# Four alternating transformer layers: logits moved from TensorE to VectorE, and the blocks ordered as a wavefront

## The chip, the cores and the metric

The kernel runs on one core of one Trainium2 chip. The metric is the device time in microseconds of one execution; the time before is the median of three runs. The profile shows one execution, whose span runs from its first to its last instruction.

## The reference

The input x has 2048 tokens of 1024 features (bf16). Four layers follow each other, A, B, A, B, with the same weights in both A and in both B layers; each adds its result to x. The core of the two:

```python
def _A_ref(x, wqkv, wo):              # x is layer-normed
    H = 32; Dh = D // H               # 32 heads of 32
    W, dil = 8, 2
    q, k, v = ...  (x @ wqkv), split by head
    idx = pos[:, None] - (arange(W) * dil)[None, :]
    ...
    logits = einsum("bhsd,bhswd->bhsw", q, kg) * Dh ** -0.5
    logits = where(idx >= 0, logits, -1e9)
    o = einsum("bhsw,bhswd->bhsd", softmax(logits), vg)
    return o @ wo

def _B_ref(x, W_gate, W_up, W_down):  # F = 3584
    return (relu(x @ W_gate) * (x @ W_up)) @ W_down
```

Each token looks at itself and at seven earlier ones, two tokens apart, in each of 32 heads.

## The kernel before

x stays in SBUF as 16 tiles of 128 tokens. The work is cut into 4 blocks of 512 tokens (BLK), four tiles each, and goes layer by layer, block by block within a layer: 16 items (L, b). `merge` interleaves the steps of an item with those deferred from earlier items by fractions of the item (SCHED 3), and the framework turns the result into one instruction stream per engine, each of which runs in order. All loads of weights, transposes and round trips are issued on SyncE (SP), whose queue waits in order too.

An A item has 24 projections `proj(c, q|k|v)`, each 8 matmuls of 128x128 by 128x512 into one PSUM bank (L316), copied to SBUF by ScalarE (ACT). q and k stay on chip with features on the partitions. For each chunk c of 128 features VectorE (DVE) multiplies q by k at the eight shifts in one instruction of 4096 elements (L345), and `red(c)` sums over the features of each head on TensorE (PE): eight matmuls with a stationary matrix `wide` of ones (L358), into a two-bank PSUM tile. The softmax is on DVE and ACT (L373 to L382). Only v goes out to DRAM (`v_d`) and comes back head-major (`vhm`, L428): 32 heads by four groups of 128 tokens on the partitions, 32 features and 142 tokens along the row. `pv(g)` (L440 to L443) forms the weighted sum of v on DVE for four features at a time. Its result goes out to `o_d` and comes back as `oT`, for wo (L471), whose result DVE adds to x (L478). wqkv is loaded once per block, in rows of 512 B (L302).

A B item has 28 steps `gu(j)`: eight matmuls for the gate, relu by ACT into one of three buffers r (L518), eight matmuls for up (L513), and on DVE the product of the two, hT (L519). Then come 224 down matmuls (L543), and DVE adds their sums to x. Weights pass through a ring of five slabs of 1 MB.

Layer-norm: ACT forms the sums and the normalised rows (L186, L187, L210), DVE and GpSimd (POOL) the small steps, and one transposing DMA on SP makes xnT (L214). PSUM has six banks for matmul results and two for the logits. The numbers in names follow layer and block: hT_3_5098 is of the fourth block, block 3.

Of the kernel before, what the change touches and what calls it, by code (L numbers as in the profile page):

```python
# [11 lines left out]
AX = mybir.AxisListType  # L12
# [13 lines left out]
SLAB = 512  # L26

# [5 lines left out]
def _interleave(a, b):  # L33
    out = []
    na, nb = len(a), len(b)
    if na == 0:
        return list(b)
    if nb == 0:
        return list(a)
    ia = ib = 0  # L40
    while ia < na or ib < nb:
        if ib >= nb or (ia < na and ia * nb <= ib * na):
            out.append(a[ia]); ia += 1
        else:
            out.append(b[ib]); ib += 1
    return out
# [3 lines left out]
def kernel(  # L50
# [28 lines left out]
    import os as _os0  # L79
    _os_env = _os0.environ  # L80
# [3 lines left out]
    wring = ctx.enter_context(tc.tile_pool(name="wring", bufs=int(_os_env.get("KRING", "5"))))  # L84
    xnT_pool = ctx.enter_context(tc.tile_pool(name="xnT", bufs=2))
    ln_pool = ctx.enter_context(tc.tile_pool(name="ln", bufs=2))
    stat_pool = ctx.enter_context(tc.tile_pool(name="stat", bufs=2))
    tl_pool = ctx.enter_context(tc.tile_pool(name="tl", bufs=1))
    a_pool = ctx.enter_context(tc.tile_pool(name="attn", bufs=2))
    psum = ctx.enter_context(tc.tile_pool(name="psum", bufs=int(_os_env.get("KACC", "6")), space=bass.MemoryType.PSUM))  # L90
    psum_l = ctx.enter_context(tc.tile_pool(name="psum_l", bufs=int(_os_env.get("KLB", "1")), space=bass.MemoryType.PSUM))
# [5 lines left out]
    wide = const.tile([P, 60], BF16, name="wide")  # L97
    nc.gpsimd.memset(wide[:], 0.0)
    for hl in range(4):
        nc.gpsimd.memset(wide[32 * hl:32 * hl + 32, 28 + hl:29 + hl], 1.0)  # L100
# [4 lines left out]
    neg_half = const.tile([P, TPB], F32, name="neg_half")  # L105
    nc.gpsimd.memset(neg_half[:], -0.5)
    NTOK = HALO + S
    v_d = dram.tile([H * DH, NTOK], BF16, name="v_d")
    o_d = dram.tile([NT, H, DH, P], BF16, name="o_d")
    zpad = const.tile([P, KC, HALO], BF16, name="zpad")  # L110
    nc.gpsimd.memset(zpad[:], 0.0)
    nc.sync.dma_start(bass.AP(tensor=v_d.tensor, offset=v_d.offset, ap=[[NTOK, P], [P * NTOK, KC], [1, HALO]]), zpad[:])

    x_tiles = []
    for t in range(NT):
        xt = xpool.tile([P, D], BF16, name=f"x{t}")
        x_tiles.append(xt)
# [3 lines left out]
    def load_x_steps(b):  # L121
        def f(t):
            return lambda: nc.sync.dma_start(x_tiles[t][:], x_dram[t * P:(t + 1) * P, :])
        return [f(t) for t in range(b * TPB, (b + 1) * TPB)]

    import os as _os
    KNOB = {
        "red2": int(_os.environ.get("KRED2", "0")),
        "wo_lo": float(_os.environ.get("KWO_LO", "0.3")),
        "wo_hi": float(_os.environ.get("KWO_HI", "0.7")),  # L130
        "p2_lo": float(_os.environ.get("KP2_LO", "0.0")),
        "ln_lo": float(_os.environ.get("KLN_LO", "0.25")),
        "ln_hi": float(_os.environ.get("KLN_HI", "0.95")),
        "bq": _os.environ.get("KBQ", "sync"),
        "dt": int(_os.environ.get("KDT", "1")),
        "hp": int(_os.environ.get("KHP", "0")),
    }
    bq = {"sync": nc.sync, "act": nc.scalar, "pool": nc.gpsimd}[KNOB["bq"]]
    from contextlib import nullcontext as _nullctx

    def hp():
        return tc.high_priority() if KNOB["hp"] else _nullctx()
    _dbg_on = bool(_os.environ.get("KDEBUG"))

    def dbg(name, ap_):
        if not _dbg_on:
            return
        shp = list(ap_.shape)
        if name.startswith("ps_"):
            tmp = const.tile(shp, ap_.dtype, name=f"dbgtmp_{name}")  # L150
            nc.vector.tensor_copy(tmp[:], ap_)
            ap_ = tmp[:]
        h = nc.dram_tensor(f"dbg_{name}", shp, ap_.dtype, kind="ExternalOutput")
        nc.sync.dma_start(h.ap(), ap_)
# [8 lines left out]
    def lnt_steps(item):  # L163
        L, b = item
        holder = {}
        steps = []

        def alloc():
            holder["xnT"] = xnT_pool.tile([P, TPB, KC, P], BF16, tag="xnT", name=f"xnT_{L}_{b}")
            holder["st"] = stat_pool.tile([P, 2, TPB], F32, tag="st", name=f"st_{L}_{b}")  # L170

        def stats(t):
            def f():
                if t == 0:
                    alloc()
                    if KNOB["dt"]:
                        holder["xn_all"] = ln_pool.tile([P, TPB, D], BF16, tag="xn_all", name="xn_all", bufs=1)
                st = holder["st"]
                xt = x_tiles[b * TPB + t]
                if KNOB["dt"]:  # L180
                    junk = holder["xn_all"][:, t, :]
                    junk2 = junk
                else:
                    junk = ln_pool.tile([P, D], BF16, tag="junk", name="junk", bufs=1)[:]
                    junk2 = ln_pool.tile([P, D], BF16, tag="junk", name="junk2", bufs=1)[:]
                nc.scalar.activation(junk, xt[:], ACT.Identity, accum_out=st[:, 0, t:t + 1])  # L186
                nc.scalar.activation(junk2, xt[:], ACT.Square, accum_out=st[:, 1, t:t + 1])  # L187
            return f

        def small():  # L190
            st = holder["st"]
# [11 lines left out]
            holder["rstd"], holder["nb"] = rstd, nb  # L203

        def do_tr(t):
            def f():
                xt = x_tiles[b * TPB + t]
                if KNOB["dt"]:
                    xna = holder["xn_all"]
                    nc.scalar.activation(xna[:, t, :], xt[:], ACT.Identity, scale=holder["rstd"][:, t:t + 1],  # L210
                                         bias=holder["nb"][:, t:t + 1])
                    if t == TPB - 1:
                        xnT = holder["xnT"]
                        nc.sync.dma_start_transpose(xnT[:].rearrange("p t k n -> p (t k) n"),  # L214
                                                    xna[:].rearrange("p t d -> p (t d)"))
                    return
                xn = ln_pool.tile([P, D], BF16, tag="xn", name="xn")
                nc.scalar.activation(xn[:], xt[:], ACT.Identity, scale=holder["rstd"][:, t:t + 1],
                                     bias=holder["nb"][:, t:t + 1])
                tp = psum.tile([P, KC, P], BF16, tag="acc", name="tp")  # L220
                for c in range(KC):
                    nc.tensor.transpose(tp[:, c, :], xn[:, c * P:(c + 1) * P], ident[:])
                nc.scalar.copy(holder["xnT"][:, t, :, :], tp[:])
# [464 lines left out]
```

## Time and profile before

| | |
|---|---|
| time of three runs | 1686.22, 1688.92 and 1688.09 us, median 1688.09 |
| span of the profiled execution | 1682.7 us; its own time is not given apart from that, and the median of the runs is 5.4 us above it |
| granted clock of TensorE | 0.999 |
| busy: PE, DVE, ACT, POOL | 1648.5, 726.0, 452.9, 21.0 us |
| DMA engines busy, share | 64.3% of the span for the main queue |
| HBM read, written | 265.16 MB, 21.00 MB |

Read it from the engine that sets the end: busy shares say how full each engine is over the span, the strips of 40 slices say where, and the waits say who holds whom. Where an engine has much idle time in one layer and none in another, its share over the whole span tells little.

### The profile page before, as it was taken

How to read it: one execution, taken by the hardware profiler on the slowest of the kernel's cores; microseconds unless marked ns; L12 is line 12 of the kernel's file. 1: busy time of each engine (PE TensorE's matmuls, PEld its weight loads, DVE VectorE, ACT ScalarE, POOL GpSimd, SP SyncE). 2: the span in 40 equal slices, each digit the busy share in tenths (PEclk: the TensorE clock that was granted, in tenths of full speed). 3: DMA queues.
4: the chain of work that ended last, by engine and by line, in shares of the span. 5: the costliest groups of instructions: out<-in, count | busy, mean ns of one | idle time of the engine just before them, and what ended most of it. 6: DMA issues, size and time to landing. Idle time of an engine off the chain costs nothing.

```text
span 1682.7 us, 18808 instructions
## 1 busy us (share of the span) xinstructions
PE 1648.5 (98%) x7906; PEld 734.2 (44%) x7968; DVE 726.0 (43%) x873; ACT 452.9 (27%) x737; POOL 21.0 (1%) x40
## 2 busy tenths in 40 slices
PE   7999999999999999999999999999999999999998
PEld 3343434444444444444444334444444444444444
DVE  3589889562211221111135999796422112211111
ACT  6642433201410153211325335141014002300110
POOL 1000000000000000000000000000000000000000
PEclk9999999999999999999999999999999999999999
DMA  9987877854655366444759787968538455555442
GB/s 274 209 190 194 209 210 193 235 189 161 167 172 167 120 206 180 139 150 150 189 148 213 182 195 183 249 171 237 198 123 245 142 164 173 163 163 175 150 156 70
DMA packets 435013, 303.11 MB, mean 180 GB/s; under 512 B 134897, under 2 KB 429809, under 8 KB 433905
## 3 DMA queue, kind: packets, MB, share of 16 engines
q1 hardware_dynamic: 434640, 301.39, 64.3%
q8 instruction: 62, 1.02, 0.3%
q10 hardware_dynamic: 288, 0.52, 0.1%
q14 instruction: 23, 0.18, 0.0%
HBM read 265.16 MB, written 21.00 MB: 170 GB/s over the span
## 4 chain that ended last, share of the span: by engine, by line
PE 84%; DVE 7%; ACT 3%; DMA 3%; issue 2%; POOL 0%; SPq 0%; ACTq 0%; DVEq 0%; POOLq 0%
PE acc_g L513 23%; PE acc_u L513 22%; PE acc_wo L471 7%; PE acc_q L316 3%; PE acc_v L316 3%; PE acc_k L316 3%; ACT xn_all L210 1%; ACT xn_all L187 1%; ACT xn_all L186 1%; DMA xnT_2_6641<-xn_all 1%; DMA xnT_2_872<-xn_all 1%; DVE ssum L378 0%; DMA xnT_1_453<-xn_all 0%; DMA xnT_0_1818<-xn_all 0%; DMA xnT_0_7583<-xn_all 0%
## 5 line engine op out<-in xcount | busy, mean ns | idle before, releaser
L518 ACT ACTIVATE r<-acc_g 128x512 bf16<-128x512 f32 x224 | 132.7, 594 | 829.2 <-PE acc_g L513 797.8
L519 DVE TENSOR_TENSOR hT_3_10875<-acc_u,r 128x512 bf16<-128x512 f32 x28 | 19.4, 692 | 77.4 <-PE acc_u L513 77.4
L519 DVE TENSOR_TENSOR hT_3_5098<-acc_u,r 128x512 bf16<-128x512 f32 x28 | 19.4, 692 | 77.4 <-PE acc_u L513 77.4
L519 DVE TENSOR_TENSOR hT_1_8821<-acc_u,r 128x512 bf16<-128x512 f32 x28 | 19.4, 691 | 74.0 <-PE acc_u L513 69.1
L519 DVE TENSOR_TENSOR hT_2_9861<-acc_u,r 128x512 bf16<-128x512 f32 x28 | 19.4, 691 | 74.0 <-PE acc_u L513 69.1
L519 DVE TENSOR_TENSOR hT_1_3052<-acc_u,r 128x512 bf16<-128x512 f32 x28 | 19.4, 691 | 74.0 <-PE acc_u L513 69.1
L519 DVE TENSOR_TENSOR hT_2_4088<-acc_u,r 128x512 bf16<-128x512 f32 x28 | 19.4, 691 | 68.1 <-PE acc_u L513 56.4
L200 POOL TENSOR_TENSOR rstd<-vpe,neg_half 128x4 f32<-128x4 f32 x15 | 16.8, 1119 | 1413.7 <-DVE vpe L198 1279.7
L543 PEld LDWEIGHTS <-hT_3_10875 128*128 128x128 bf16 x224 | 21.9, 98 | 26.4
L543 PEld LDWEIGHTS <-hT_2_4088 128*128 128x128 bf16 x224 | 21.9, 98 | 26.4
L543 PEld LDWEIGHTS <-hT_0_7781 128*128 128x128 bf16 x224 | 21.9, 98 | 26.4
L543 PEld LDWEIGHTS <-hT_1_8821 128*128 128x128 bf16 x224 | 21.9, 98 | 26.4
L543 PEld LDWEIGHTS <-hT_2_9861 128*128 128x128 bf16 x224 | 21.9, 98 | 26.4
L543 PEld LDWEIGHTS <-hT_0_2016 128*128 128x128 bf16 x224 | 21.9, 98 | 26.4
L543 PEld LDWEIGHTS <-hT_1_3052 128*128 128x128 bf16 x224 | 21.9, 98 | 26.4
L543 PEld LDWEIGHTS <-hT_3_5098 128*128 128x128 bf16 x224 | 21.9, 98 | 26.4
L519 DVE TENSOR_TENSOR hT_0_2016<-acc_u,r 128x512 bf16<-128x512 f32 x28 | 19.0, 686 | 28.3 <-PE acc_u L513 25.9
L519 DVE TENSOR_TENSOR hT_0_7781<-acc_u,r 128x512 bf16<-128x512 f32 x28 | 19.0, 686 | 28.3 <-PE acc_u L513 25.9
L358 PEld LDWEIGHTS <-wide 128*32 128x32 bf16 x512 | 9.4, 94 | 35.1 <-issue 31.6
L378 DVE TENSOR_REDUCE ssum<-d 128x128 f32<-128x1024 f32 x8 | 15.3, 1908 | 1.9 <-ACT d L376 1.9
L277 PE MATMUL tp<-ident,xn_all 128*128 128x128 bf16 x32 | 4.0, 311 | 10.0 <-DVE xn_all L255 8.7
L376 ACT ACTIVATE d<-d 128x1024 f32<-128x1024 f32 x8 | 8.5, 1058 | 14.6 <-DVE d L375 14.6
(1513 smaller groups left out, 3291.3 us busy)
## 6 DMA issues: line engine op xcount, KB each, us to landing
vhm_0_734<-v_d SPq DMA_DIRECT2D x4, 284.0 KB, 7.1
vhm_1_1664<-v_d SPq DMA_DIRECT2D x4, 284.0 KB, 7.4
vhm_2_2287<-v_d SPq DMA_DIRECT2D x4, 284.0 KB, 8.9
vhm_3_3323<-v_d SPq DMA_DIRECT2D x4, 284.0 KB, 9.9
vhm_0_6503<-v_d SPq DMA_DIRECT2D x4, 284.0 KB, 6.7
vhm_1_7429<-v_d SPq DMA_DIRECT2D x4, 284.0 KB, 6.7
vhm_2_8052<-v_d SPq DMA_DIRECT2D x4, 284.0 KB, 8.3
vhm_3_9092<-v_d SPq DMA_DIRECT2D x4, 284.0 KB, 10.4
```

What stands on the lines that cost most here:

```text
L186: nc.scalar.activation(junk, xt[:], ACT.Identity, accum_out=st[:, 0, t:t + 1])
L187: nc.scalar.activation(junk2, xt[:], ACT.Square, accum_out=st[:, 1, t:t + 1])
L200: nc.gpsimd.tensor_tensor(rstd[:], vpe[:], neg_half[:], op=ALU.pow)
L210: nc.scalar.activation(xna[:, t, :], xt[:], ACT.Identity, scale=holder["rstd"][:, t:t + 1], bias=holder["nb"][:, t:t + 1])
L316: nc.tensor.matmul(acc[:], lhsT=wsl[:, kc, wcol:wcol + P], rhs=xnT[:, :, kc, :], start=(kc == 0), stop=(kc == KC - 1))
L358: nc.tensor.matmul(Lt[32 * tq:32 * tq + 32, 4 * wh:4 * wh + 4, :], lhsT=wide[:, 28 - 4 * c:60 - 4 * c], rhs=prod[:, 4 * wh:4 * wh + 4, tq ...
L378: nc.vector.tensor_reduce(ssum[:], d[:].rearrange("p w t -> p t w"), axis=AX.X, op=ALU.add)
L471: nc.tensor.matmul(acc[:], lhsT=oTa[:, c, t, :], rhs=wsl[:, c, :], start=(c == 0), stop=(c == KC - 1 and not res_pe))
L513: nc.tensor.matmul(acc[:], lhsT=slabs[nm][:, kc, jl * P:(jl + 1) * P], rhs=xnT[:, :, kc, :], start=(kc == 0), stop=(kc == KC - 1))
L518: nc.scalar.activation(r[:], acc[:], ACT.Relu)
L519: nc.vector.tensor_tensor(hT[:, j, :], accs["u"][:], r[:], op=ALU.mult)
L543: nc.tensor.matmul(ac[t], lhsT=hT[:, j, t * P:(t + 1) * P], rhs=wsl[:, jl, :], start=(j == 0), stop=(j == FC - 1))
```

## The change

The kernel is written anew around the same tiles. In the diff:

- q, k and v are all staged by ACT (`stage`, two buffers of two chunks), stored to DRAM per block (`q_d`, `k_d`, `v_d`; the last 14 tokens also into the next block's rows), and read back head-major (`load`, L292: four DMAs each).
- The logits are on DVE alone: for each shift w one multiply of 4096 elements (`mul`) and a tree of six adds with f32 results over the 32 features (`tree`). `wide`, `red` and their 512 matmuls go, and with them the two PSUM banks: eight banks are now for matmul results.
- The max and the sum of the softmax are trees of three instructions in place of one reduction each.
- `Plan` sorts all steps by planned times, kept by a clock for PE (`plan.pe`, 0.216 us a matmul) and one for DVE (`plan.dve`). The order on PE is a wavefront: the projections of layer 0, with wo(0,0) in the middle of the last; then for each b gate_up(1,b), wo(0,b+1) or wo(2,0), down(1,b) and, from b = 1, proj(2,b-1); then gate_up(3,0), proj(2,3), wo(2,1), down(3,0), gate_up(3,1), wo(2,2), down(3,1), gate_up(3,2), wo(2,3), down(3,2), gate_up(3,3), down(3,3).
- In layer 0 the six 1 MB slabs of wqkv are loaded once and stay in the ring (`w0`), which now has six buffers. In layer 2 they are loaded per block, in rows of 1 KB.
- xnT and oT share one pool `tpose` of three buffers.

The core of the diff (`+` is the changed kernel, `-` the one before):

```diff
-    wring = ctx.enter_context(tc.tile_pool(name="wring", bufs=int(_os_env.get("KRING", "5"))))
+    wring = ctx.enter_context(tc.tile_pool(name="wring", bufs=6))
+    tpose = ctx.enter_context(tc.tile_pool(name="tpose", bufs=3))
+    psum = ctx.enter_context(tc.tile_pool(name="psum", bufs=8, space=bass.MemoryType.PSUM))
...
-        def red(c):
-            def f():
-                prod = st.pop(("prod", c))
...
-                        nc.tensor.matmul(Lt[32 * tq:32 * tq + 32, 4 * wh:4 * wh + 4, :],
-                                         lhsT=wide[:, 28 - 4 * c:60 - 4 * c],
...
+    def plan_proj(plan, L, b, ready, between=None):
...
+                    if L == 0:
+                        if b == 0:
+                            w0[(nm, g)] = load_slab(wqkv_v[:, :, col0:col0 + SLAB], f"w{nm}_{L}_{g}")
+                        hold["w"] = w0[(nm, g)]
...
+                nc.scalar.copy(s[:, j % 2, :], acc[:])
+                if j % 2 == 1:
...
+                    if nm == "q":
+                        dst = _dram(q_d[b], f0 * BLK, [[BLK, P], [P * BLK, 2], [1, BLK]])
+                        nc.sync.dma_start(dst, s[:])
...
+    def plan_attn(plan, L, b, ends, pace):
+        def load(nm, src, row, n):
+            def f():
+                t = hm_pool.tile([P, DH, n], BF16, tag=nm, name=f"{nm}hm_{L}_{b}")
+                for tq in range(TPB):
+                    nc.sync.dma_start(t[32 * tq:32 * tq + 32, :, :],
+                                      _dram(src[b], tq * P, [[DH * row, H], [row, DH], [1, n]]))
...
+        def mul(w):
...
+                nc.vector.tensor_tensor(pr[:], st["q"][:], _ap(st["k"], HALO - DIL * w, [[HALO + P, DH], [1, P]]),
+                                        op=ALU.mult)
...
+        def tree(w):
+            def f():
+                pr = st.pop(("pr", w))
+                l1 = at_pool.tile([P, 8, P], F32, tag="l1", name="l1")
+                nc.vector.tensor_tensor(l1[:], pr[:, 0:8], pr[:, 8:16], op=ALU.add)
+                nc.vector.tensor_tensor(l1[:], l1[:], pr[:, 16:24], op=ALU.add)
+                nc.vector.tensor_tensor(l1[:], l1[:], pr[:, 24:32], op=ALU.add)
+                for n in (4, 2):
+                    nc.vector.tensor_tensor(l1[:, 0:n], l1[:, 0:n], l1[:, n:2 * n], op=ALU.add)
+                nc.vector.tensor_tensor(st["L"][:, w, :], l1[:, 0], l1[:, 1], op=ALU.add)
...
+        q0 = max(ends["k"] + 0.5, plan.dve - 45.0)
+        plan.at(q0, load("q", q_d, BLK, P))
+        plan.at(q0, load("k", k_d, ROW, HALO + P))
+        plan.at(max(ends["v"] + 0.5, plan.dve), load("v", v_d, ROW, HALO + P))
+        t = max(plan.dve, ends["k"] + T_BOUNCE)
+        for w in range(0, W, 2):
+            plan.at(t, mul(w))
+            plan.at(t + 2.2 * pace, mul(w + 1))
+            plan.at(t + 4.4 * pace, tree(w))
+            plan.at(t + 9.0 * pace, tree(w + 1))
+            t += 13.6 * pace
...
+    for b in range(NB):
+        if b + 1 < NB:
+            ln(0, b + 1, [plan.pe + 14.0 + 2.6 * t for t in range(TPB)])
+        proj(0, b, between=(lambda: wo(0, 0)) if b == NB - 1 else None)
+    for b in range(NB):
+        gate_up(1, b)
+        if b + 1 < NB:
+            wo(0, b + 1)
+        else:
+            wo(2, 0)
+        down(1, b)
+        if b >= 1:
+            proj(2, b - 1)
+    for b in range(NB):
+        gate_up(3, b)
+        if b == 0:
+            proj(2, NB - 1)
+        if b + 1 < NB:
+            wo(2, b + 1)
+        down(3, b)
+    plan.run()
```

`gu`, `down`, `wo`, `pv` and the layer-norm keep their instructions; the hT multiply is now L437, the adds to x L400 (wo) and L464 (down), r still has three buffers.

## The prediction

> **What bounds the kernel now.** I read the page's first, second and fourth parts, then windows by stage, then the waits, then the rows that price the new work.
>
> ```profile
> PE 1648.5 (98%) x7906; PEld 734.2 (44%) x7968; DVE 726.0 (43%) x873; ACT 452.9 (27%) x737; POOL 21.0 (1%) x40
> ...
> PE   7999999999999999999999999999999999999998
> ...
> DVE  3589889562211221111135999796422112211111
> ...
> DMA  9987877854655366444759787968538455555442
> ...
> PE 84%; DVE 7%; ACT 3%; DMA 3%; issue 2%; POOL 0%; SPq 0%; ACTq 0%; DVEq 0%; POOLq 0%
> ```
>
> TensorE sets the time: 98% busy and 84% of the chain. VectorE is full only in slices 2 to 8 and 20 to 27 of 40, the two attention layers, and idle in between. The windows answer says the same with numbers (columns: stretch, length, busy of PE, PEld, DVE, ACT, POOL, clock, DMA share, GB/s):
>
> ```profile
> 100.00:140.00 40.00, 37.81 (x201) 16.12 (x194) 40.00 (x34) 11.14 (x19) 0.00 (x0) 1.00 0.88 203
> ...
> 380.00:860.00 480.00, 478.84 (x2208) 217.35 (x2229) 96.78 (x158) 117.87 (x190) 5.04 (x5) 1.00 0.54 163
> ```
>
> In attention both engines are full; in the GLU layer PE misses 1.2 us of 480. The waits say why PE is not held there: VectorE waits for PE at all 28 hT multiplies, never PE for it.
>
> ```profile
> DVE hT_3_5098 L519 <- PE acc_u L513: 77.4, 28, 3.1
> ...
> PE acc_g L513 <- DMA xnT_0_1818<-xn_all: 2.2, 1, 2.2
> ```
>
> **TensorE's floor.** Eight matmuls of 512 columns take 1.73 us in the chain, 0.216 each. The 7424 that stay make 1604 us: a projection block 41.5, wo 13.8, gate_up 96.8 (28 steps j of 3.456), down 48.4. With the start (first matmul at 15.05, its first eight 3.56, so 16.9 in effect) and 4.1 after the last one: 1625. The span of before is 1682.7: some 35 more for the 64 logit reductions (PE's busy 1648.5 less 1604, less 4.0 of transposes and 5 of the slow start; 0.55 each) and 23 of waits. The change takes the 35 away; that is its sure gain, and the waits could go too. The medians of the shown runs lie 5.4 above this span; I add 5.4 to every span, supposing that what lies around it stays.
>
> **What VectorE gets.** Rows of before:
>
> ```profile
> L345 DVE TENSOR_TENSOR prod_251<-q_237,k_0_0_248 x1: 2293/2293/2293, 21.8 to 21.8; 128x4096 bf16<-128x4096 bf16 x1
> ...
> L375 DVE TENSOR_TENSOR d<-L_0_305,m x1: 1224/1224/1224, 68.2 to 68.2; 128x1024 f32<-128x1024 f32 x1
> ...
> L382 DVE TENSOR_TENSOR a_0_631<-d,rs x1: 1224/1224/1224, 75.3 to 75.3; 128x1024 bf16<-128x1024 f32 x1
> ...
> L441 DVE TENSOR_TENSOR t_800<-t_800 x1: 1217/1217/1217, 106.3 to 106.3; 128x2048 bf16<-128x2048 bf16 x1
> ...
> L519 DVE TENSOR_TENSOR hT_3_5098<-acc_u,r 128x512 bf16<-128x512 f32 x28 | 19.4, 692 | 77.4 <-PE acc_u L513 77.4
> ```
>
> One offset w costs a 4096 multiply as before (2.2 from start to start), and now a tree: three adds of 1024 with an f32 side, then f32 adds of 512, 256 and 128. 1024 and 512 have rows (1.22, 0.69); the line through them gives 0.43 and 0.29. With 0.03 for each start behind its own result the tree is 5.2 and the offset 7.45. The first add (bf16 in, f32 out) has no row: it lies between 0.68 (the 1024 bf16 add) and 1.22; I take 1.22 by L382, the nearest mixed form; the other end saves 8 x 0.54 = 4 us a block. The Trainium skill, "VectorE: DVE Perf Modes", "What auto-detection actually checks", speaks against the f32 tree: the double rate needs every tensor 16-bit. By it 1.22 holds and the sum stays; against it, 4 a block would go.
>
> Per block: 8 x 7.45 = 60, softmax 8 (3.7 of trees, subtract, reciprocal 0.95, multiply, the wait for exp), pv 8 x 4.27 = 34: 100 to 102, bounds 95 and 104. Before it was about 60. The total rises from 726 to about 1060 us, 63% of the span: enough room on average, so the question is where it lies.
>
> **Where it lies.** VectorE runs in order. In the built program each attention of blocks (0,1) to (2,2) stands inside one gate_up phase, between its hT multiplies; down and projection have 12.6 us of VectorE in 90. From the first hT multiply to the last, gate_up offers 27 x 3.456 = 93.3. VectorE's rows there sum to 98.7 in (1,0), 104.4 in (1,1), 120 in (1,2), (1,3) and (3,0), and 18.5 in (3,2) and (3,3), with 92 ahead of the first hT in (3,1). TensorE cannot run on: r has 3 buffers and PSUM 8 banks, so it leads by four j, 14 us, and then waits.
>
> For (1,2), (1,3), (3,0), T being the start of the projection before: its k load stands on SP behind the transpose of the next layer-norm, whose buffer (three shared by xnT and oT) comes free with the projection's last matmul, T + 41.5. The queue rows:
>
> ```profile
> 66.93 7.78 SPq L214 DMA_TRANSPOSE xnT_2_872<-xn_all  x1
> 74.80 5.08 SPq L428 DMA_DIRECT2D vhm_0_734<-v_d  x4
> ...
> vhm_0_734<-v_d SPq DMA_DIRECT2D x4, 284.0 KB, 7.1
> ```
>
> 7.8 for the transpose, 5.1 for four loads, 7 to land: k is there at T + 63. hT1 to hT4 are done by then; from there to hT24 the rows sum to 104 (between hT8 and hT9 alone 27.5), so T + 167; u28, which needs hT24's bank, ends at T + 168.5 instead of T + 138.3. With attention at 100 rather than 102, +29 each; if k is never late, VectorE starts after hT4 at T + 55: +20; with later loads +36.
>
> Layer 0 is alike. Before starts gate_up(1,0) at 224; the floor is 16.9 + 4 x 41.5 + 13.8 = 196.6. Attention (0,0) waits for k stored (chunks end 44.6, landing 8), 10 us of queue for q and k and 7 to land: 67, so it ends about 168, beside layer-norm steps. o out (4.0), oT back (6.6) and what SP has between (some 10) put wo(0,0) at 190, ending 204. (PE is free from about 179: the floor's 162 for three and a half projections, and 17 lost in block 1, where the layer-norm step of block 3 stands behind attention on VectorE, its transpose on SP, and the stores behind that.) Its residual adds stand behind seven offsets of attention (0,1), 168 + 52 = 220; the eight banks hold wo's sums, so the last half of proj(0,3) (20.7) waits for them: 241, then the layer-norm transpose: gate_up(1,0) at 250, bounds 235 and 260: +53 (+38 to +63).
>
> The rest: (1,0) starts 8 late on VectorE and has 5 too much: +8 (3 to 12). (1,1): 11 too much, hT1 up to 11 late, less a lead: +15 (8 to 20). (3,1): attention (2,3) starts 7.5 after wo(2,1); 92 us stand before hT1, 25 more to hT8, which frees the bank of j = 12: 121 to 125 against 90 at the floor: +30 (20 to 38).
>
> Weights: wqkv in layer 0 goes three times less over DMA (3 x 12288 packets of 512 B at 32 ns, over 16 engines: 74 us), 1-KB rows in layer 2 save 23; the q and k round trips add 21 a block (by the packet records: 4096 of 256 B at 22 ns and as many of 284 B at 34, 2048 of 1 KB at 52, over 16): 168. Net +71, to some 1150 busy of 1820: off the path on average. ACT's copies stay equal in number; each of 0.59 hides beside 1.73 of matmul; if not, 24 a block would come.
>
> **Sum.** 1625 + 53 + 8 + 15 + 3 x 29 + 30 = 1818 span, 1823 as a time. Low ends: 1625 + 38 + 3 + 8 + 60 + 20 + 5 = 1759; high ends: 1625 + 63 + 12 + 20 + 108 + 38 + 5 = 1871.
>
> **Rivals.**
> *VectorE keeps ahead* (faster). If hT multiplies are served in time, PE loses the reductions and most waits: 1625 + 15 to 25 in layer 0 + 5 = 1645 to 1655. For it: 63% of VectorE on average. Against: the order is fixed, and 120 does not fit into 93 plus a lead of 14. It decides if attention takes under about 80 a block. 0.12.
> *Only part of the lateness reaches PE.* Layer 0 as forecast at its low end, the three phases at 5 to 15, (3,1) absorbed: 1700 to 1759. For it: the lead may be longer, and k may land before hT4. 0.17.
> *The queue starves PE.* Stores that wait for ACT or VectorE block SP, and slabs come late in all of layers 1 to 3, as in the window of 88% DMA share: 2 us at each of the 35 slab pairs of the five gate_up phases that hold attention adds 70: 1893, spread 1871 to 1940. For it: all of it on SP, 256-B packets. Against: 54% share in GLU. The Trainium skill, "DMA: Bandwidth & Descriptors", "Specifications", says that packets under 512 B miss the line rate, the direction of these rows (22 ns for 256 B, 52 for 1 KB). Chance 0.10.
> *Gains and losses cancel*: 0.02. Forecast, 1759 to 1871: 0.59.
>
> A measurement of this kernel tells about 0.2% from no change. Range 1725 to 1895, which leaves out the fast case, the near end of the second and the far end of the third. Faster 0.12, same 0.02, slower 0.86.
>
> **What would show it.** Right: PE's strip dips in gate_up of (1,2), (1,3), (3,0); waits of acc_u or acc_g on the hT multiply or relu, near 30 us a phase; no idle VectorE from k's landing to hT28; gate_up(1,0) near 250; attention about 100 of VectorE a block. The layer-0 step is wrong if wo's adds are not late; the forecast is wrong if PE is over 95% busy, or if PE waits for slabs rather than for VectorE.

## The result, and the profile after

The changed kernel takes 1822.91 us (median of four runs, 1821.95 to 1825.6); the kernel before takes 1687.15 (median of four, 1685.18 to 1688.92). The ratio is 1.0808, with a 95% interval of 1.0793 to 1.0823: slower by 136 us. The forecast was 1823, range 1725 to 1895.

The profile page of the changed kernel, the parts that were shown of before (busy time, strips, chain):

```profile
PE 1640.1 (90%) x7407; PEld 734.8 (40%) x7456; DVE 1024.4 (56%) x1225; ACT 447.2 (25%) x737; POOL 20.8 (1%) x35
...
PE   7779689969899987999879998799679999999999
...
DVE  1599988989991049920599105991896211221111
...
DMA  9848688646857695476953969539837465456541
...
PE 61%; DVE 27%; DMA 4%; issue 3%; ACT 2%; SPq 2%; POOL 0%; DVEq 0%; POOLq 0%; ACTq 0%
```

TensorE falls from 98 to 90% of the span, and its share of the chain from 84 to 61%; VectorE's rises from 7 to 27%. VectorE's strip shows five separate hills (slices 2 to 12, 15 to 17, 20 to 22, 25 to 27 and 29 to 31), and TensorE's strip dips at each. After slice 32 VectorE is nearly idle and TensorE full: there is no attention left. VectorE is busy 56% on average, so its share of the span explains nothing.

The windows answer of the changed kernel, for gate_up(1,2) with its attention and for a stretch without attention (columns as before: stretch, length, busy of PE, PEld, DVE, ACT, POOL, clock, DMA share, GB/s):

```profile
645.00:766.00 121.00, 100.96 (x450) 44.43 (x449) 103.70 (x113) 19.10 (x32) 0.00 (x0) 0.93 0.71 169
...
1512.00:1768.00 256.00, 255.69 (x1182) 115.84 (x1187) 51.23 (x78) 46.71 (x76) 1.01 (x1) 1.00 0.52 161
```

The waits of TensorE in the changed kernel (engine, what waited, releaser: us in total, times, longest):

```profile
PE acc_u L432 <- DVE hT L437: 38.3, 8, 11.3
PE dacc L458 <- DMA wd<-in_B_W_down_dram: 32.6, 2, 17.5
PE acc_u L432 <- DMA wu<-in_B_W_up_dram: 19.8, 5, 7.7
PE acc_g L432 <- DVE x L464: 11.9, 1, 11.9
PE acc_k L253 <- ACT stage_k L255: 11.4, 1, 11.4
PE acc_k L253 <- DVE x L400: 9.4, 1, 9.4
...
PE acc_g L432 <- DMA xnT<-xn_all: 8.7, 1, 8.7
PE acc_g L432 <- DMA wg<-in_B_W_gate_dram: 7.3, 1, 7.3
```

Before, TensorE hardly waited for anyone in GLU; now it does, and for two parties of like weight. Over the whole kernel, what VectorE releases late (hT, x, and 6.9 put down to the tree at L311) is 66.5 us; weight slabs that land late (wd, wu, wg, and 6.1 for wo) are 65.8. The 6.9 is probably a slab too: it ends 8.5 us after the issue of wu, at the place in (1,3) where (1,2) and (3,0) end their waits for wu 8.9 and 8.6 us after its issue. Then it is 59.6 for VectorE and 72.7 for slabs. Staging by ACT adds 20.5, the transpose 8.7.

### The profile page after: what moved, and what is told of

The parts are those of the page before. It is cut to its first block, busy times and chain, and to the rows that moved or that the text cites. A ratio compares the mean times of both kernels' runs of the same rounds, so it can differ in the third digit from the quotient of the medians.

```text
span 1820.3 us, 18488 instructions
## 1 busy us (share of the span) xinstructions
PE 1640.1 (90%) x7407; PEld 734.8 (40%) x7456; DVE 1024.4 (56%) x1225; ACT 447.2 (25%) x737; POOL 20.8 (1%) x35
## 2 busy tenths in 40 slices
DMA packets 468277, 319.07 MB, mean 175 GB/s; under 512 B 216288, under 2 KB 460000, under 8 KB 468192
## 4 chain that ended last, share of the span: by engine, by line
PE 61%; DVE 27%; DMA 4%; issue 3%; ACT 2%; SPq 2%; POOL 0%; DVEq 0%; POOLq 0%; ACTq 0%
PE dacc L458 17%; PE acc_u L432 15%; PE acc_g L432 14%; DVE pr L302 5%; PE acc_wo L397 4%; PE acc_q L253 4%; PE acc_k L253 3%; DVE l L312 3%; DVE l L313 3%; DVE l L311 3%; PE acc_v L253 3%; DVE pvt L349 3%; DVE l L315 3%; DVE hT L437 2%; DMA khm<-k_d 1%
## 5 line engine op out<-in xcount | busy, mean ns | idle before, releaser
L432 PE MATMUL acc_u<-xnT,wu 128*128 128x512 bf16 x1792 | 435.8, 388 | 65.1 <-DVE hT L437 38.3
L432 PE MATMUL acc_g<-xnT,wg 128*128 128x512 bf16 x1792 | 429.9, 384 | 27.9 <-DVE x L464 11.9
L458 PE MATMUL dacc<-wd,hT 128*128 128x512 bf16 x1759 | 390.5, 382 | 34.5 <-DMA wd<-in_B_W_down_dram 32.6
L437 DVE TENSOR_TENSOR hT<-acc_u,r 128x512 bf16<-128x512 f32 x224 | 153.7, 687 | 348.6 <-PE acc_u L432 348.6
L432 PEld LDWEIGHTS <-wu 128*128 128x128 bf16 x1792 | 177.1, 99 | 289.0 <-issue 56.2
L458 PEld LDWEIGHTS <-hT 128*128 128x128 bf16 x1792 | 175.8, 98 | 247.8 <-issue 23.1
L432 PEld LDWEIGHTS <-wg 128*128 128x128 bf16 x1792 | 176.6, 99 | 245.6 <-issue 30.8
L464 DVE TENSOR_TENSOR x<-dacc,x 128x512 bf16<-128x512 f32 x64 | 43.4, 690 | 223.7 <-PE dacc L458 223.7
L302 DVE TENSOR_TENSOR pr<-qhm,khm 128x4096 bf16<-128x4096 bf16 x64 | 145.7, 2286 | 17.6 <-DMA v_d<-stage_v 10.4
L349 DVE TENSOR_TENSOR pvt<-a,vhm 128x4096 bf16<-128x4096 bf16 x64 | 145.6, 2287 | 0.2
L253 PE MATMUL acc_k<-xnT,wk 128*128 128x512 bf16 x512 | 117.4, 389 | 27.6 <-ACT stage_k L255 11.4
L400 DVE TENSOR_TENSOR x<-acc_wo,x 128x512 bf16<-128x512 f32 x64 | 42.8, 688 | 66.5 <-PE acc_wo L397 66.5
L313 DVE TENSOR_TENSOR l<-l,pr 128x1024 f32<-128x1024 f32 x64 | 78.4, 1225 | 2.0
L312 DVE TENSOR_TENSOR l<-l,pr 128x1024 f32<-128x1024 f32 x64 | 78.2, 1223 | 1.6
L311 DVE TENSOR_TENSOR l<-pr 128x1024 f32<-128x1024 bf16 x64 | 78.3, 1223 | 1.6
```

Of the source, the lines that this page charges most:

```text
L253: nc.tensor.matmul(acc[:], lhsT=w[:, kc, j * P:(j + 1) * P], rhs=xnT[(L, b)][:, :, kc, :], start=(kc == 0), stop=(kc == KC - 1))
L302: nc.vector.tensor_tensor(pr[:], st["q"][:], _ap(st["k"], HALO - DIL * w, [[HALO + P, DH], [1, P]]), op=ALU.mult)
L311: nc.vector.tensor_tensor(l1[:], pr[:, 0:8], pr[:, 8:16], op=ALU.add)
L312: nc.vector.tensor_tensor(l1[:], l1[:], pr[:, 16:24], op=ALU.add)
L313: nc.vector.tensor_tensor(l1[:], l1[:], pr[:, 24:32], op=ALU.add)
L349: nc.vector.tensor_tensor(tt[:], a_bc, v_sh, op=ALU.mult)
```

## The experiments

My theory: VectorE's order puts a whole attention in front of the hT multiplies, and TensorE stops for them. The rival: SP's queue, which holds all reloads, stores, transposes and weight slabs in one order, starves TensorE, and VectorE is only one of the things that SP waits for. All edits are against the changed kernel unless another is named; ratios are to the kernel before, which took 1685.1 to 1686.4 in the same jobs.

**VectorE in the plan's order.**

```diff
-    plan.run()
+    with tc.manual_schedule(engines={mybir.EngineType.DVE}):
+        plan.run()
```

The plan has a time for every step. The built program of the change doesn't keep VectorE to it; this edit does.

> The plan is run in a region in which VectorE keeps the order of the plan (in the changed kernel the framework's scheduler had moved attention forward into gate_up). Same instructions. VectorE's rows from the first to the last hT multiply sum to 103 in gate_up(1,0), 99 in (1,1), 104 in (1,2), (1,3) and (3,0), where they were 99, 104 and 120. Theory 'place' (attention stands inside gate_up on an engine that runs in order): the three phases go from +24.5 to about +15 each, layer 0 gains up to 10: 1785, between 1770 and 1805. Rival 'queue' (weight slabs stand behind waiting entries of SP): no phase gains, 1810 to 1825.

Measured: 1781.43 us, 1.0572 [1.0553, 1.0591], 41.5 less. The three phases (1,2), (1,3), (3,0) last 107 to 109 each, where they lasted 121 to 122, and the waits for hT shrink from 38.9 to 4.6 us in all. The waits for slabs stay (wd 26.3, wg 15.1). What is left in the three phases, 10 to 12 us each, is mostly a wait for ACT's last copies of v (22.0 in three waits): they need a staging buffer, whose store stands on SP behind the transpose and the reload of k. Waits for staging are 56 us in this run, against 20.5.

**The same, with attention spread over the phase.** The pace of the plan's attention goes from 1.15 to 2.0 after layer 0.

```diff
-        attn[(L, b)] = plan_attn(plan, L, b, ends, 1.0 if L == 0 and b == 0 else 1.15)
+        attn[(L, b)] = plan_attn(plan, L, b, ends, 1.0 if L == 0 and b == 0 else (1.15 if L == 0 else 2.0))
...
-    plan.run()
+    with tc.manual_schedule(engines={mybir.EngineType.DVE}):
+        plan.run()
```

> As the run in the plan's order, and layer 2's attention at pace 2.0 in place of 1.15, so that it is spread over gate_up, wo, down and projection: rows in gate_up(1,2), (1,3), (3,0) sum to 71 of 93.3, with 62 in down and projection. Same instructions, same total on VectorE. Place: no waits for hT multiplies are left in these phases (-12 to -16 each beyond the run before), and down(3,0) and gate_up(3,1) lose most of their 33: 1745, between 1715 and 1765. Rival 'amount' (VectorE simply has too much to do): as the changed kernel, over 1800. Rival 'queue': the slab waits of 7.5 in three gate_up phases and 17 in down(1,0) and down(3,0) stay, 1780 to 1800.

Measured: 1753.15 us, 1.0409 [1.0393, 1.0424], 28 less again. In the waits of this run the hT multiply is gone from TensorE's list:

```profile
PE dacc L458 <- DMA wd<-in_B_W_down_dram: 27.2, 3, 17.7
PE acc_k L253 <- ACT stage_k L255: 21.2, 2, 20.8
PE acc_g L432 <- DMA wg<-in_B_W_gate_dram: 15.5, 1, 15.5
PE acc_u L432 <- DMA wu<-in_B_W_up_dram: 14.0, 3, 6.3
```

So 70 us come back with not one instruction fewer on VectorE. Slab waits are 65.9 us (with 9.2 for wo), as large as in the change, and they are now what GLU loses most by. (Some 43 us over the floor still lie in layer 0. The longest wait there, 20.8 for staging, arises because ACT stands 23.6 us for a layer-norm step of VectorE, with the copies behind it.) SP's timeline of the same run shows how the two longest arise (start, length, queue entry):

```profile
280.37 11.42 SPq L354 DMA_DIRECT2D o_d<-ohm  x2
291.88 0.39 SPq L137 DMA_DIRECT2D wg<-in_B_W_gate_dram  x1
...
420.99 9.64 SPq L354 DMA_DIRECT2D o_d<-ohm  x2
430.72 0.39 SPq L137 DMA_DIRECT2D wd<-in_B_W_down_dram  x1
```

SP stands at two outputs of pv that VectorE has not made yet, 34 us in all at the first place and 23 at the second; right behind them stands the slab that TensorE waits 15.5 and 17.7 us for.

**One add in place of the tree.** The logits are then sums of two features only, and VectorE has about 37 us less a block (731 us in all, against 1024).

```diff
-                nc.vector.tensor_tensor(l1[:], pr[:, 0:8], pr[:, 8:16], op=ALU.add)
...
-                nc.vector.tensor_tensor(st["L"][:, w, :], l1[:, 0], l1[:, 1], op=ALU.add)
+                nc.vector.tensor_tensor(st["L"][:, w, :], pr[:, 0], pr[:, 1], op=ALU.add)
```

> Leaves out the sums over the 32 features: each logit is the sum of two products, one add of 128x128 in place of the tree's six; all else as in the changed kernel. Attention takes about 60 of VectorE a block in place of 100, below the 80 that the prediction gave as the point from which VectorE keeps ahead. Place and amount: no waits for hT multiplies, gate_up(1,0) at 205 to 215, about 1680, between 1660 and 1705. Queue: the slab waits stay or grow, since PE asks for weights sooner: 1720 to 1780.

Measured: 1721.94 us, 1.0218 [1.0198, 1.0238]: 101 less, but some 40 short of what I expected. gate_up(1,0) starts at 220.4 in place of 250.2. The waits of this run:

```profile
PE acc_u L426 <- DMA wu<-in_B_W_up_dram: 21.9, 5, 7.3
PE dacc L452 <- DMA wd<-in_B_W_down_dram: 19.7, 2, 17.4
PE acc_k L253 <- ACT stage_k L255: 12.3, 1, 12.3
...
PE acc_u L426 <- DVE hT L431: 7.6, 8, 2.8
PE acc_g L426 <- DMA wg<-in_B_W_gate_dram: 7.2, 1, 7.2
```

hT falls from 38.3 to 7.6, the slabs only from 65.8 to 51.9 (with 3.1 for wo). One slab wait goes with VectorE's load: wd in down(1,0) falls from 15.05 to 2.3. The others hardly move: wd in down(3,0) is 17.4 (17.5 in the change), wg 7.2 (7.3), wu 6.0 to 7.3 at the place where it was 6.9 to 7.7. Making VectorE light is not enough, and most of the slab waits are not VectorE's doing.

**Stores of q, k, v on ACT's queue.**

```diff
-                        nc.sync.dma_start(dst, s[:])
+                        nc.scalar.dma_start(dst, s[:])
```

(and so at the other two stores of the staged chunks)

> The stores of q, k and v (with the halo) are issued on ScalarE's queue, not on SP. Place: the waits for ACT's staging copies in projection blocks 1 and 2 (18 in all) go, but wo(0,0) still starts near 190, since it waits for attention (0,0) on VectorE: -0 to -10, 1813 to 1823. Queue: SP, freed of entries that wait for ACT, brings weights and k earlier in all phases: -30 or more, under 1795.

Measured: 1841.71 us, 1.0929 [1.0907, 1.0951]: 19 slower, not faster, against both theories. The waits for staging go, but SP's timeline of this run shows what moved up, in the phase of (1,2):

```profile
668.74 7.00 SPq L292 DMA_DIRECT2D vhm<-v_d  x4
675.78 1.66 SPq L137 DMA_DIRECT2D wu<-in_B_W_up_dram  x1
```

The whole reload of v, 7.0 us of the queue, now comes ahead of the slab wu, which is issued 19.2 us after the start of this gate_up, where it was 14.2; TensorE waits 11.9 to 13.9 for wu in each of the three phases. In layer 0 the same reload stands ahead of a transpose, with 20.8 us of waits for xnT. So relief for a queue can cost time, where what is left moves up into a worse order.

**Reloads and outputs of attention on GpSimd's queue**, on top of the spread order:

```diff
-                    nc.sync.dma_start(t[32 * tq:32 * tq + 32, :, :],
+                    nc.gpsimd.dma_start(t[32 * tq:32 * tq + 32, :, :],
...
-                    nc.sync.dma_start(_dram(o_d[b], (g - 1) * DG * P, [[DH * P, P], [1, 2 * DG * P]]),
+                    nc.gpsimd.dma_start(_dram(o_d[b], (g - 1) * DG * P, [[DH * P, P], [1, 2 * DG * P]]),
...
-                nc.sync.dma_start(oT[:, :, tq, :], _dram(o_d[b], tq * H * DH * P, [[P, P], [P * P, KC], [1, P]]))
+                nc.gpsimd.dma_start(oT[:, :, tq, :], _dram(o_d[b], tq * H * DH * P, [[P, P], [P * P, KC], [1, P]]))
```

> As the spread run (1753), with what waits for attention issued on GpSimd's queue and not on SP: the head-major loads of q, k, v, the stores of o and the loads of oT. Left in the spread run are waits of PE for weight slabs, 15.5 in gate_up(1,0), 17.7 in down(1,0), 8.4, 6.3 and 6.0 in gate_up(1,2), (1,3), (3,0), 9.6 in down(3,0). Queue theory (SP's entries wait for VectorE's o and for reloads, and the slabs stand behind them): most of these 63 go, with the slow matmuls behind each: 1695, between 1685 and 1720. If these waits were DMA bandwidth, or VectorE in another form: 1740 to 1760.

Measured: 1706.77 us, 1.0129 [1.0114, 1.0144], 46 below the spread order alone. The waits of this run: of the slabs only 3.4 us for wg and 1.4 for wu are left; xnT in layer 0 (24.8) and staging (16.4) come first now.

```profile
PE acc_q L253 <- DMA xnT<-xn_all: 24.8, 2, 12.9
PE acc_g L432 <- ACT stage_v L255: 15.8, 5, 4.8
...
PE acc_g L432 <- DMA wg<-in_B_W_gate_dram: 3.4, 1, 3.4
```

**A fourth buffer for the transposes**, on top of the spread order, paid for with one product buffer in place of two (multiply and tree then take turns).

```diff
-    tpose = ctx.enter_context(tc.tile_pool(name="tpose", bufs=3))
+    tpose = ctx.enter_context(tc.tile_pool(name="tpose", bufs=4))
```

> As the spread run (1753), with four buffers for xnT and oT in place of three; the room comes from one buffer in place of two for the products, multiplied and summed in turn. The transpose in front of the k load no longer waits for the last matmul of the projection. The step of the prediction: in gate_up(1,2), (1,3) and (3,0) k lands 10 or more earlier, and the slab waits of 8.4, 6.3, 6.0 with their slow matmuls go: 1730, between 1720 and 1742; the waits in (1,0), down(1,0) and down(3,0) stay. If the transpose's buffer is not what holds SP: 1748 to 1760.

Measured: 1757.69 us, 1.0426 [1.0411, 1.0442]: not faster than the 1753.15 with three buffers. The slab waits remain (wg 33.9, wu 21.3, wd 9.7). In (1,2) the edit does what was expected of it: the load of k goes out 2.8 us before gate_up starts, where it went out 5.8 after, and the phase loses 2.9 us in place of 10.2. But TensorE waits 18.9 us for wg ahead of gate_up(1,1), and (1,3) loses 14.0 in place of 8.7. So the buffer does hold k back, as the prediction said, but the total gains nothing; since the edit also takes a product buffer, what the buffer alone is worth stays open.

**The same order with the tree in bf16** (five adds of 2048, 1024, 512, 256 and 128 elements in place of six with f32 sums; rounding of the sums differs).

> As the spread run (1753), with the tree's adds in bf16 (2048, 1024, 512, 256 elements, and the last into f32): by the rows 1.22, 0.68, 0.41, about 0.3 and 0.2, 2.8 in place of 5.2 an offset, so attention takes about 82 a block. Place and queue: layer 0 gains what attention (0,0) gains, 15 to 20, and o's stores, for which SP waits, come earlier; 1725, between 1710 and 1738. Amount: the whole 8 x 18 comes off, under 1650.

Measured: 1736.35 us, 1.0305 [1.029, 1.032], 17 less. The rows of the adds are 1216, 692, 425, 292 and 292 ns. Slab waits of 56 us remain (5.1 of them for wo): a quarter of the 68 us that were left goes with VectorE's speed, the rest stays.

**wqkv loaded per block in layer 0 again**, everything else as changed:

```diff
-                    if L == 0:
+                    if L == 0 and False:
```

> The changed kernel (1823), but wqkv is loaded for each block of layer 0 again, 1 MB slabs in rows of 1 KB: 18 MB more, about 60 us of 16 engines in the first 250, where they are 72% busy. If DMA bandwidth holds layer 0: k and the stores later, +10 to +25. If attention (0,0) on VectorE holds it: within 5 of 1823.

Measured: 1861.88 us, 1.1041 [1.1022, 1.1059]: 39 slower than the change. The windows answer over layer 0, up to the start of gate_up(1,0), of this run:

```profile
16.00:290.00 274.00, 197.86 (x829) 84.77 (x829) 194.97 (x213) 102.32 (x174) 5.28 (x4) 0.87 0.84 211
```

and of the changed kernel:

```profile
16.00:250.00 234.00, 189.20 (x829) 82.97 (x829) 177.73 (x200) 101.73 (x174) 4.91 (x4) 0.93 0.72 169
```

gate_up(1,0) starts at 290.3, 40 later. TensorE waits 34.3 us for wq, a line that the waits of the changed kernel don't have, and the DMA share is 0.84 against 0.72. This part of the change is worth 39 us, more than either expectation gave it; the prediction had it off the path. In the longest wait for wq, 17.1 us, SP issues the slab only 7.9 us after TensorE has begun to wait, behind reloads and stores, and it lands about 9 later. How much the fuller DMA adds to that was not taken apart.

**Plan's order and GpSimd's queue without the spread** fills the square:

> The run in the plan's order (1781), with the reloads of q, k, v, the stores of o and the loads of oT on GpSimd's queue, as in the spread run with that queue (1707), but without the spreading: VectorE's rows sum to 104 in gate_up(1,2), (1,3), (3,0) again. It completes a square of two (spread or not, queue free or not): 1781, 1753, 1707 and this. Place counts for itself: waits for hT multiplies of 5 to 12 in each of the three phases and a few in (3,1), 1737, between 1722 and 1755. Place reaches PE only by way of SP's queue: 1705 to 1718.

Measured: 1722.95 us, 1.0216 [1.02, 1.0231]: just inside the range of place, without its waits of 5 to 12 a phase. TensorE waits 5.4 us for hT in gate_up and 7.4 before wo, and 19.3 for the adds to x.

| | reloads on SP | reloads on GpSimd |
|---|---|---|
| plan's order | 1781.4 | 1723.0 |
| plan's order, spread | 1753.2 | 1706.8 |

The queue is worth 58 and 46, the spread 28 and 16. The spread gives 12 less once the queue is free, as it would if part of its gain were that SP is blocked for a shorter time.

**Layer 0.** More than half of what was left lay there (gate_up(1,0) starts at 240.7 in the last cell of the square, 44 us over its floor), and three runs went after it. The first, on top of the last cell of the square: layer-norm steps of layer 0 planned earlier (offsets 14, 3 and -18 us from the projection before), earlier loads of x, attention (0,0) planned for a start 30 us after k, its v load 25 after v, four staging and five r buffers, one product buffer, GpSimd in plan order too.

```diff
-            ln(0, b + 1, [plan.pe + 14.0 + 2.6 * t for t in range(TPB)])
+            ln(0, b + 1, [plan.pe + (14.0, 3.0, -18.0)[b] + 2.6 * t for t in range(TPB)])
...
-        t = max(plan.dve, ends["k"] + T_BOUNCE)
+        t = max(plan.dve, ends["k"] + (30.0 if (L, b) == (0, 0) else T_BOUNCE))
```

> The spread run with GpSimd's queue (1707), and: layer 0's layer-norms planned before attention (0,0) on VectorE, with x loaded earlier, so that their steps don't stand behind it; GpSimd in the plan's order too; one buffer for the products, and with the room four staging buffers in place of two, five r in place of three. Arithmetic as in the changed kernel. Layer 0: PE's waits for xnT in blocks 2 and 3 go, wo(0,0) still waits for attention (0,0): gate_up(1,0) at 225 in place of 241. The waits for staging copies in gate_up(1,3) and (3,0), 7 to 8 each with slow matmuls, go: 1668, between 1655 and 1688, faster than before. If wo(0,0) comes no earlier, 1680 to 1690.

Measured: 1710.62 us, 1.0147 [1.013, 1.0164]: a miss by 43. Later phases lose little, but layer 0 got worse: gate_up(1,0) starts at 258.6, after 47.3 us in which TensorE waits for oT. The second run takes the bf16 tree as well:

> As the run before it (e10), with the tree's adds in bf16. On the path only attention (0,0) gets shorter, by 18, if it is what wo(0,0) waits for: 1652, between 1642 and 1672. If layer 0 is held by PE or by the queue: as e10.

Measured: 1677.31 us, 0.9947 [0.9932, 0.9962], again above what was expected. VectorE's timeline of this run shows a cause of both misses:

```profile
111.30 0.17 DVE L161 TENSOR_SCALAR mean<-st 128x4 f32<-128x4 f32 x1 [26.34 <-ACT xn_all L154]
```

VectorE, held to an order, stands for 26 us at the layer-norm step of block 3, which I had moved ahead of attention, because ACT makes its sums only then. In the run before it stands 19.5 us at the same step; that is not the whole of its miss. An order that is written out must be right about every engine that it waits for. The third run puts that step back (offset 3) and ACT, too, into the plan's order:

```diff
-            ln(0, b + 1, [plan.pe + (14.0, 3.0, -18.0)[b] + 2.6 * t for t in range(TPB)])
+            ln(0, b + 1, [plan.pe + (14.0, 3.0, 3.0)[b] + 2.6 * t for t in range(TPB)])
...
-    with tc.manual_schedule(engines={mybir.EngineType.DVE, mybir.EngineType.Pool}):
+    with tc.manual_schedule(engines={mybir.EngineType.DVE, mybir.EngineType.Pool, mybir.EngineType.Activation}):
```

(and a pace of 0.8 for attention (0,0))

> As e11 (1677), where VectorE stood 29 us in attention (0,0) before the layer-norm step of block 3, whose sums ScalarE had not yet made, and 8 us before exp: that step is planned 21 us later, ScalarE runs in the plan's order too, and attention (0,0) is planned at pace 0.8. If these stalls are what wo(0,0) waits for, they go: attention (0,0) ends near 165, gate_up(1,0) starts at 215 to 220 in place of 246, 1650, between 1640 and 1663. If ScalarE in the plan's order holds PE up in the phases, it gives that back: 1665 to 1690.

Measured: 1659.85 us, 0.9838 [0.9825, 0.9851]: 1.6% below the kernel before, the best version, and 163 us below the change as made. gate_up(1,0) starts at 226.2, later than the 215 to 220 expected. Three things changed at once here (the step, ACT's order, the pace), and no run tells them apart. Its page:

```profile
PE 1614.8 (97%) x7456; PEld 731.1 (44%) x7456; DVE 915.8 (55%) x1161; ACT 457.9 (28%) x737; POOL 141.1 (9%) x195
...
PE   7899599999999999999999999999999999999999
...
DVE  1098769988987045564556635565555664211211
...
q0 software_dynamic: 13824, 43.79, 12.3%
```

From slice 15 on VectorE's hills are flat, 3 to 6 tenths throughout the phases with attention, and behind its start TensorE has one dip, in slice 5: 16.6 us for oT before wo(0,0). Its sums are in bf16; with f32 sums, the best that was run is 1706.77.

## Why the prediction came out, point by point

**The sum.** The span is 1820.3 where 1818 was forecast. TensorE's floor holds: it stays near 1625, and the stages without attention run at it. What was added to it, by stage (an undisturbed gate_up of this run takes 96.7 us, down 48.35):

| term | forecast | measured |
|---|---|---|
| start of gate_up(1,0) over its floor | 53 | 53.6 (250.21) |
| gate_up(1,0) | 8 | 8.8 |
| gate_up(1,1) | 15 | 9.6 |
| down(1,0) | 0 | 17.5 |
| gate_up(1,2), (1,3), (3,0) | 29 each, 87 | 24.3, 24.6, 25.2: 74.1 |
| down(3,0) | 0 | 19.4 |
| gate_up(3,1) | 30 | 13.5 |
| sum | 193 | 196.5 |

The total is off by under 4, but 35 us lie in gate_up phases that were forecast too high, and 37 in two down stages that were forecast at nothing. That the number came out is therefore in part luck. By causes it is the same: outside layer 0 the forecast put every loss down to VectorE; in the list of waits VectorE releases 50 to 57 us there, late slabs 60 to 67. The 5.4 us taken for what lies around the span is 1.9 in the profiled run.

By the signs that the prediction set itself, these came: the dips of TensorE's strip, no idle VectorE from k's landing to the end of the phase, gate_up(1,0) near 250, and attention near 100 of VectorE a block (102.3 from the first step to the last in block (0,0), the steps of a layer-norm included). "Near 30 us a phase" for hT did not come: it is 10 to 11. Of the two signs of being wrong, TensorE is not over 95% busy, and it waits for slabs as much as for VectorE.

**The three phases** were reasoned in the right order of events, and over-priced. SP's timeline for (1,2), whose T is 603.7:

```profile
645.37 4.84 SPq L179 DMA_TRANSPOSE xnT<-xn_all  x1
...
650.95 4.94 SPq L292 DMA_DIRECT2D khm<-k_d  x4
...
659.41 0.59 SPq L137 DMA_DIRECT2D wu<-in_B_W_up_dram  x1
```

and VectorE's:

```profile
662.60 4.50 DVE L302 TENSOR_TENSOR pr<-qhm,khm 128x4096 bf16<-128x4096 bf16 x2 [2.65 <-DMA khm<-k_d]
```

The transpose comes at T + 41.7 (forecast T + 41.5), k at T + 59 (forecast T + 63), and from there to T + 162 VectorE is busy 100.6 of 103 us, as forecast. The transpose's start goes by its buffer, as the run with a fourth one bears out in this phase, though that run gained nothing in all. But the form of the loss differs; TensorE's timeline shows three waits:

```profile
668.35 3.60 PE L432 MATMUL acc_u<-xnT,wu 128*128 128x512 bf16 x8 [7.47 <-DMA wu<-in_B_W_up_dram]
...
686.88 1.90 PE L432 MATMUL acc_u<-xnT,wu 128*128 128x512 bf16 x8 [2.45 <-DMA wu<-in_B_W_up_dram]
...
710.87 3.21 PE L432 MATMUL acc_u<-xnT,wu 128*128 128x512 bf16 x8 [10.00 <-DVE hT L437]
```

Ten for hT, ten for slabs that SP issued behind its transpose, reload and stores, and about 4 of slower matmuls behind the waits, a term that the prediction didn't have. Since VectorE is busy up to the end of the phase, the slab wait inside it probably cost nothing more; no run took the slab waits away and left VectorE as it was. The other way round is shown: with VectorE's lateness gone, in its own order or with the tree out, 10 to 12 us a phase remain.

**(1,1) and (3,1)** had their amounts put down to VectorE alone. In gate_up(1,1) TensorE never waits for hT; its 9.6 us are a wait of 7.3 for a slab wg and the slow matmuls behind it. The larger losses are waits for slabs wd, 15.05 in down(1,0) and 17.5 in down(3,0). SP's timeline before the first:

```profile
361.14 4.80 SPq L292 DMA_DIRECT2D khm<-k_d  x2
394.82 4.86 SPq L179 DMA_TRANSPOSE xnT<-xn_all  x1
...
401.15 3.03 SPq L137 DMA_DIRECT2D wd<-in_B_W_down_dram  x2
```

and TensorE's at the wait:

```profile
409.18 26.32 PE L458 MATMUL dacc<-wd,hT 128*128 128x512 bf16 x110 [15.05 <-DMA wd<-in_B_W_down_dram]
```

From 366 to 394.8 SP stands at a transpose. Its layer-norm waits for VectorE's adds to x, which end only at 381, between the steps of pv, and for small steps of VectorE up to 390; then wd goes out, too late. SP's timeline before the second, and ACT's:

```profile
1266.34 0.45 SPq L137 DMA_DIRECT2D wd<-in_B_W_down_dram  x1
1284.40 1.32 SPq L264 DMA_DIRECT2D v_d<-stage_v  x2
...
1295.06 13.60 SPq L137 DMA_DIRECT2D wd<-in_B_W_down_dram  x6
```

```profile
1278.79 4.64 ACT L175 ACTIVATE xn_all<-x,nb,rstd 128x1024 bf16<-128x1024 bf16 x4 [1.80 <-DVE nb L170]
1283.33 2.00 ACT L255 CAST stage_v<-acc_v 128x512 bf16<-128x512 f32 x4
```

Here SP stands 17.5 us at a store of v, for a copy that ACT makes only at 1283.33: in ACT's order it stands behind the whole layer-norm of the next block. VectorE is not late; from 1260 to 1278 it does little but wo's adds, each as TensorE delivers it. The tree-out run agrees: this wait stays with a light VectorE, the first one goes. (The wait also gave VectorE time, so what gate_up(3,1) would have lost without it stays open.)

This is the step that failed: the prediction put the weights at nothing ("off the path on average") and priced VectorE's lateness only along the hT multiplies. In its place the runs show 65.8 to 72.7 us of waits for slabs behind entries at which SP stands: rows that VectorE has delayed (down(1,0)), a copy that ACT makes late (down(3,0)), a buffer that TensorE frees and the reloads and stores behind it (the three phases). It is the "queue starves PE" rival, which I gave 0.10, in a different shape: not a full DMA (0.55 of the engines' time from 355 to 409, 0.75 from 1272 to 1304) and not 2 us at every slab pair, but a few long waits, each behind one blocked entry.

**Layer 0** met its sum, 250.21 against 250, and its adds were late as said: the projection restarts at 219.23 after 9.35 us for x (L400), forecast 220. Block 1 lost 16.2 us, where 17 were forecast for SP's queue. The path was ACT's order, and so it was in block 2, which lost another 8.2:

```profile
87.95 4.64 ACT L175 ACTIVATE xn_all<-x,nb,rstd 128x1024 bf16<-128x1024 bf16 x4 [5.86 <-DVE nb L170]
92.50 2.01 ACT L255 CAST stage_k<-acc_k 128x512 bf16<-128x512 f32 x4
```

ACT waits for a layer-norm step that VectorE makes amid attention, and the copies of k, for which TensorE waits 11.4 us, stand behind it; later copies of v, waited for 5.6, stand behind the exp of attention (0,0), whose input VectorE makes late. So TensorE came to wo(0,0) only at 187.6 (forecast 179), and what it waited for there was not oT but the slab of wo, 6.1 us, issued behind oT's loads. That wo(0,0) starts near its forecast all the same, 193.7 against 190, is partly luck.

**The rows** chosen for the tree hold: 1223 ns for the bf16-to-f32 add of 1024 (forecast 1.22), 690, 419 and 290 for 512, 256 and 128 (0.69, 0.43, 0.29). By "VectorE: DVE Perf Modes" of the Trainium skill, section "What auto-detection actually checks", the mixed add gets no double rate; the trace agrees (1223 ns, where a bf16 add of 1024 elements takes 685). From start to start an offset takes 7.37 (forecast 7.45) and a step of pv 4.28 (4.27). VectorE's total is 1024 us where about 1060 was forecast.

**Small slips that change little.** The terms given for k's landing add up to T + 61.4 and not T + 63, those for the start of attention (0,0) to 69.6 and not 67 (VectorE starts it at 65.2). 24 copies of 0.59 are 14 us and not 24; the sum did not use them. The second hill of VectorE's strip before is slices 22 to 28, not 20 to 27.

**Still open:** what the slab waits alone would cost with VectorE late as in the change; how the loss inside layer 0 divides between staging, transpose and adds (no run changed one of them alone); and whether the order on SP is all that makes the stores on ACT's queue slower, since ACT's own later work was not taken apart.

## What to carry to other kernels

Price added work on an in-order engine where it stands in the order, stage by stage, and follow each late result to everyone who waits for it: the matmul's bank, and also the queue in which an entry that waits for it blocks the weight loads behind it. Do the same for the engine that copies results out of PSUM: here copies stood behind a layer-norm or an exp, and TensorE or SP waited for them. When prefetches share a queue with entries that wait for computed data, put one of the two kinds on another engine's queue; here that was worth 46 to 58 us (with fewer packets, see below), and keeping the planned order on VectorE and spreading it another 70, with no instruction removed. An order written out by hand must be right about every engine that it waits for: VectorE in the plan's order gained 41 us, but a step put ahead of what ACT had ready stopped it for 20 to 26.

## What the hardware showed besides

**After a long wait TensorE's matmuls run slower for a while, which costs 1 to 3 us more.** Eight matmuls start 1.73 us apart in steady running, and show as about 1.9 us with their ends. After the 2.45 us wait shown above they take 1.90, so nothing; after waits of 7.47 and 10.00 they take 3.60 and 3.21, and the eight behind the first of these 2.33. After a wait of 4.37 us they take 3.18; the windows over that place show the granted clock (the last three columns: clock, DMA share, GB/s):

```profile
342.20:345.50 3.30, 3.22 (x9) 1.18 (x9) 3.27 (x4) 0.60 (x1) 0.00 (x0) 0.58 0.00 0
345.50:350.00 4.50, 4.50 (x22) 2.05 (x21) 4.43 (x7) 1.09 (x2) 0.00 (x0) 1.00 0.49 129
```

0.58 for the first 3.3 us, 1.00 after. "TensorE: Matmul & The Clock Gate" of the Trainium skill, in its part on the clock gate, puts the fall to half rate at an idle window of about 3.4 us and the return at as long a busy one; the trace agrees at these two places, none after 2.45 and one after 4.37. Taken over all fourteen traces (waits of 0.9 us and more behind the first 20 us, without those of the logits), the limit is less sharp: the clock falls after none of 38 waits under 2 us, after 21 of 43 between 2 and 4, the shortest 2.06, and after all 106 over 4. After those the slow matmuls add 1.0 to 2.9 us. Over the kernel TensorE is busy 1640.1 us where the last run needs 1614.8 for the same matmuls (49 of the 7456 records are missing in the first): about 25 us, a term that any estimate of waits should have.

**Reloads issued by GpSimd move the same bytes in fewer packets.** The last run has 344374 packets in all where the change has 468277, for 319.08 and 319.07 MB; its queue q0 carries 43.79 MB in 13824 packets, 3.2 KB each on average, in 12.3% of the 16 engines' span. GpSimd is busy 141 us for it, against 20.8. How much of the 46 to 58 us comes from the packets, and how much from the order on SP, no run separates. "DMA: Bandwidth & Descriptors" of the Trainium skill, section "Issuing engines are not separate DMA queues", holds that several issuers save only issue time; in this kernel the waits that vanish are those of the slabs, 65.9 us in the spread order and 4.8 with GpSimd's queue, which speaks for what no longer stands behind a blocked entry.
